# Another recorded order of the same items in a fused attention and two-layer kernel, and the warm-up matmuls in another PSUM bank

## The chip, the cores and the metric

The kernel runs on one core of a Trainium2 chip, as one program. The metric is the device time of one execution in microseconds (us); lower is better. PE is the matrix engine (TensorE), PEld its weight loads, DVE the vector engine, ACT the scalar engine, POOL is GpSimd, and SP is the engine that issues the DMAs.

## What is computed

Two steps follow each other. First attention with a hash mask, for 2 batches of 8 heads, 768 positions, 64 values a head:

```python
q_bits = (einsum('bhsd,dk->bhsk', q, proj) > 0)      # 6 bits a row, k_bits likewise
mask = q_bucket[:, :, :, None] == k_bucket[:, :, None, :]
scores = where(mask, matmul(q, k.T) / 8, -1e9)
attn = exp(scores - max(scores)); attn = attn / (sum(attn) + 1e-9)
x = matmul(attn, v)                                  # as 1536 rows of 512
```

Then two dense layers, each with weights of 512x2048 and 2048x512: `h = x @ w_in`, a pointwise `g(h)` (a clipped square in the first, `h - tanh(h)` in the second) and `x = g @ w_out`. The weights are wide (64 bits a value) in device memory and are made narrow in the kernel.

## The kernel before, in words

The 768 positions stand in two halves of 384 columns (SH). A query tile is 128 rows, so a group (one head, one half) has three tiles, and there are 96 tiles t, 48 for each batch. For one tile PE makes the scores with four matmuls of 384 columns (emit_s, lines 506 and 510), DVE takes their minimum (L524; the sign of the scores is turned) and makes bias and scale (L525), ACT makes the exponential and its sum (L526). Then the result is split into a high and a low fp16 part (L531 on ACT or DVE, L532 on POOL or L533 on DVE), a DMA transposes both (L537), and PE multiplies with V (pv, L631). For 18 of the 96 tiles PE itself transposes (turn, L593, evicted by L601) and multiplies in fp32 (L621). Each head's keys and queries are scaled and split before (L297 to L307), and their hash bits come from small matmuls into the bank PB, compared by DVE (first_k: L381, L382, L385; later heads L398, L399, L402; queries L412, L413, L416).

Every fp32 product is made of three matmuls with rounded operands: high by high, high by low, low by high. So each dense operand is split too: the high part by a copy on ACT or DVE (L300, L797, L815), the low part by a subtraction on POOL or DVE (L306 or L307, L798 or L799, L816 or L817). Raw weights are made narrow by L786 to L789. The dense products are L866 (bank pair MM); for batch 1 a Strassen-like form makes some from seven smaller products (products, L897, with sums on DVE L902 and weight sums on POOL or DVE, L811 or L810).

Nothing is issued while the program is being described. Every operation is put into a list (Plan.op) with the engines that may do it, and a recorded table, SCHEDULE, holds for each of the 3,456 items its place in the order and its engine. Plan.unpack reads the table, checks that no item stands before one that it depends on, and Plan.emit then issues the items in that order:

```python
for lo, hi in zip(code[:n], code[n:2 * n]):
    i = left.pop(lo + 256 * hi)
return out, [c[x][0] for x, (c, _) in zip(code[2 * n:], self.ops)]
```

Each engine works through its own items in that order and waits by semaphores for the others. Among the items are 64 that compute nothing (spin, L1127, here called spin items): four matmuls each of a constant tile `warm` into the unused last 128 columns of a PSUM bank, `WT` (L198). They keep PE busy where the order expects it to wait. The plan itself knows no dependency for them, but the framework puts a wait before a spin when another engine still works on the bank that it writes.

Of the kernel before, what the change touches and what calls it, by code (L numbers as in the profile page):

```python
# [20 lines left out]

SPINS = 64
SCHEDULE = (
    "c-rk)YjB*^d4At>Ki~bb`|Yk)yV_l8S6baAOO`Cz@)cw3*aXWsHsBbjiNO%sLP89QjlmcaJ7q!x851X5len&dB$Hd)q?sX^PEvO|40O_z>2xOf(LW_^r_-5E"
    "JMAz%qOL7lEA6@^{ZpUS=-WMe&Ux?8`<%UQ$H#CpZd<bxZr^wiuj98u2KVos`3JF?dYqyyNqQ5aW_grYwFp6{+p**|HPFCC&dvznUJPa0UIJ3EAnQsEX`8@A"
    "IgZ|)gfRJ!M2$hphpc$F9h^4)TdArM@opD{fDyK1C+@2_0<v9iJA3%!-M}D*H~A;aM2*>sWE>zVOqi0eC8Ds22ns7#G8<Q%rQ<K*@-wh{{KYftXHcve9mW;g"
    "c=EebQv^N$Y3DlFF!scHo7AcV)GccIk#*(D3X~v<Fgyuz2)dRnqlH|(t9>xrk)7%7g-ot{_np~bB$Gg8WFQ$TLuyaI*B{6A#EZJ)THG~+^_5--y+P5hwpF_P"
    "vgi999(Rpp%m#2#VLp^P&csQZ-WsJOrX3jw>V@2eh=qTc5{^&7w;TeN!u0RURPOZITq>X#dTHV#rP}`zc<}5=AG~M&w9OM)Ip^aPs6UQ=V2u9(p-}`5k=ASS"
    "ZqLIzU1cJ3M%%V{S0Q;(I{$Qs1Dx;H{G`Giw*>)v2Dxi<YFQ5fJxGZF6p>(TrI?<EbyIu|pZw7z`KbKia(U|tL_P{*y8_&~lLCS5+u4TzEHb;buSS4BCq7pZ"
    "9Pq@66R?h)1GXL?d-BQ0)_wNq41MIpr}5b1_(Jln%wx<!`jBN=IF1KL)EV{i5JmFN^Zod=Jb>bhpA!Igd=}{OrzrnR`XrM-|JgA{Pw+?I0Cw~U*+mZh<okzz"  # L30
    "N?vDx`0w9^2g#fN0-yLM0=)K*uWh}Ly~F<gSAWC&*WmPNAP)H@y!7%fQNv%W7vMSgDSV0ZXMfD`b)-74>7StfBP8;BKa_~y#x^E|2@#N2XrjJOT}jDV{#BVG"
    "v3!X|<X1HKazM$RFNWU9;OCCZeR%8bw>)s)c*D|fdiGzq=kmXB?YI8y+=N3X>_7jBH3lTDQiLogg!td*^t<vq4za&S`FDu0m=^6^r&tc~v>^OzuYQeyI4!6R"
    "ER!KhQJ2CqC-Lus;3XgQKf6Fq5YSxVqYl&7!=Mgv`>zg5{<a47Np7;3;Qa#bi}}3|5O|&5b@yFJ9AK_Ax%UZEkSN)!;`e}}5O4skXRl`(_9?m<$TpA?opxbU"
    "i$n4uBBf2mqvFUDhX{wQ?BLDAyJ6xtsUD!}qi{F>V0{|4_Uv={+B%GnGgv;=X{u#8fx*(qNP9;g(wUKd93s7wNJw?xShY$fMmhn<%h*pk0AOGYYJGXw(pBs3"
    "ht7eS^&2~BXAsPkC%d3D?iQD=BCb<d=1e&GVHn5`^!7o$AA0lwtv;Z;G#jf-!UU`xQCt?~aIvpX7WjZr*)3f5?Bv}-q(nztju|PIN+Agf(2@0%cAkb5bC~fv"
    "a})!2z@#ALqgkB`mBl>(d6o*M*uQ1lH%r>)Zn!4r3Y`eh@$_}_Z<QO9Uqs{MButNnbPJ~>u==F8o+@3l>5EiMtI0_qp_oAJjld`y8FEaK^lfnyLc*QonrM~~"
    "?}KaIb8Pi$V%s!toSo(Okh|Bg^!Wa9a>ulU(b3U2#mLY0JUl1_#Xso1@gRF}N1Z*e{p0Kgs9pc8I9a_%$fuu1!S`PaNWZoB3%4Kt#y5`B+g{bLyz&`+X73YJ"
    "8Mhqq-;w-~DfEZV@(0go=IYbVQ_MDLtY6rukB3B2$;9v2?5q5U>vH`mW5ub@Xm(Thg;S@#dF*EKd3J<z{v<oZ7^tskc;H2gJg?;=>eMOqFbKhs$%70jdmhP`"
    "#qlRzApDq_Gc$OYBO*CY4O*Re+(i4+cprA*(U*_u8;*j4=Z-)I;8QHMZ5!JP=`HueJ-6IT4wz!@3SeLRBm3ZX=zxO<AJj4fABG>@&-0S+h7=EOylW&PMxQKf"
    "CL~R;L#7dWxts;Did;W+%f_3N6|l?X{7tqU1Be}KW>v1XVe_6<>SoAH*%Gwc&31+D>_%vtis*EHQ+7po4QvR=_$cu@NKAt2Y_(1x*Ipe#kjrHW+I#gnSX=L*"  # L40
    "P^(b_HJ5kcGD<UK2z~<x3WZ*5kIT2!?(3=XS`BL)DxE;fG}qx!VmYa9TFbKZ`lyl~U^68`ix2hm&=MIO8%r1a6^*k4lydG<B7JICpxohbLNq0-dUMk527yK1"
    "HR9v$e7P)wAWJw_>-DK>wmX*@&oEZ0*eG?cq&@P62~SGesVlbD9r37MTQHpfbCMzNz7q*lDw{QQaUsgtk`SwNg0Dpur7~El#2P!4GTk=s4i|tE+aU%36%bJ>"
    "Bd5Z3x4I9cMAb`7gNzN91>luDTNWf*)0P00a27!*=@f($qumfFpRu7sI7rz|gS&dD=`Khr1VtzIr4VSkP^If=re}2zlrue1S5k~pseALiP-u&fLR(kVxnV=5"
    "vJTdF!$c|AIUej7D{kLW8ihj955w@|klhO|)ZiZIhJT%??LPodDeGg)0Dl__L-!69B&^T(5zc4&R`vBrIbECNhc}qd#<k~WT;Rh~4%y85`uk9i)-?`K4J$Q>"
    "<3eLy?Z=@_ID2?-BV9uW2JU1lKY}y#+9_J!OAbtQ6aJBLj$>?e#oo~oN{8s+ZFs9U?Cn`&s80`0+w~px<mg1T8^NhKlfzDFMDJQQtVgWbVQY3^I}FtO1_A1u"
    "px1P{YSFap4n|6)0wtu4lt*(pPBK9IFqfoo?p2R_qwW;eieXgg?2Iag7*(KX3Z&#Y09hN71Xh`<qQFfD6ls~3Aq44&`zosYA+NfcJKRE<S8YmZrBo`LS80@7"
    "q-n%y;4tc1j^i0R$F!D8qs&PZ8dBvn=Mc50ISW}pJ#YrV$TU1g)v1K`GReQ!Q_2YWG+;W;#c`CxkwMuuqZuVC3>8>5IF@6&kM@<9^%P4(-fp871Tpb#&nGSf"
    "j;~$Yu?<I2R)C4}QYd`@-{qkpE}q$oz0?4dFo|UPbdE5P#x*fPq)}TNgjs_!BISb1jft)?(sh-#yFisvN=J&ZwhljANTm`;On+k#QAFhi<-qMA9j;5-^Jw#|"
    "rI|@@#(~WQEP#~`owRKry%sZ&VhRsvi2)^y8uKVZWc(dEX!|Mi)DH6k+b}n`2v)n52Q<(wvPmY%WRiqt5?W&bot+p20YV}4JP)$5n;2q<9%^DE8s@>TH6}5F"
    "WF6v+39DgtuAwm0A|5gA$r?89HxvNO>2uNch-(&uVU<QVW+n_3jwxm!4$$yGQ;=xQt(L|t-X`YAtw}RlCJq+SNuya|1yK|*UouZvMPY-sG-Xm59t13*X$Hhl"  # L50
    "5#Nwa-}8Kp#<vxargumQl4lK20%SsPGa-SL?L}aPuH##C=LC-HxZuPZXg&zEZ@^rn(hj6zWU&Dp&lu%sXD;qe-X^&uYoP(7x%>mqP`gRPNCnknCbz2w)}WU`"
    "r)j4oA-u#4NeztAZs6uz&rL84(ILkF1``Zu87@>PF!SPhEV`7=C82SH38o|5lI;{7*F~Po=`1P(pQcqvCp66qCaD9$upe_Y<E%yu|1-Nu(fAl47eYQrXcDB9"
    "$xtsS#-0_n1)-7eDo~bD6y``gc$P~&i)t{jF_>ex6)<8>GHHtx&^0$08!VuP(51~58k*yc+U6gbi#QnIo%>|w%$314Sv~id`-8dn_}<*y<oR*&-Nh+){x_E_"
    "a4$ZcxrcM%8)x1sXW^O7lHWF3{$GFKII!5sO++?0)mc=jD>>%9f$(b`b_>Gs%2c!87h~-A%fbsXt^e%-^Cxhrx2=k^&abkXY<X{8YwGJoXZ4jV*DZTTUs$ah"
    "o~+^j(LlI5uDb5(xH_(mtK;gpI{vSlsA;2!O&V+SR!dsw*4XOWr4GQ$H6qxA9N;DQ5_~^MMe|kIx}5pf0Bn2^F1{UG(is;9{rpb+pV&DsXK=yA4;NU2i^pZr"
    "ELlu7T;N@7e9>wxScuJngN+nNSlq-$G8USRja0w}(Y;iSD~)zb&OltMTpMi1X7_z;APp~+FfQ1J3sba}pBJ!!1F@CR<K+&(#r%tlI0-M!)g{A^3lGJm0?;fe"
    "mq;#bHT@Ci#|ak~j;&`~gKTZhMGbs<Q4?%bhKnO&OYy(N{00)Sp;k+{23x7m#z^1tJ+`^+7bIYFzhk3t<HDkCgeI4#87>OXOBW=zn&#MAoUfp68rqAv1ovtE"
    "_XeB~cIP1vFEsK7c+fy8Yz@2dN=g(P5dp-7-4qd9X)_2*TXM0Qu;ET@X!ueNM{I#xK@&2CczMxcGlDRmg<%7df(sJma;}Q=LWNBuh6vcgs>a@JhO6gYfQ`}}"
    "F9|&^lAG8J=kUKpG@!EButPTIPuQ%-Hn8TrDwhKUVpE^~n#X?vH%h1Q"
)  # L60


# [65 lines left out]
def lsh_attention_moe_kernel(ctx: ExitStack, tc: tile.TileContext, qT, kT, vR, projR, eye, w1, w2, w3, w4, out, nbits):  # L128
    nc = tc.nc
    B, H, D, S = qT.shape  # L130
# [42 lines left out]
    P = [pall[:, i * S:(i + 1) * S] for i in range(3)]  # L173
# [17 lines left out]
    PV = bufs("pv", 1, [128, 512], F32, psum)  # L191
    PB = bufs("pb", 1, [128, 512], F32, psum)
# [11 lines left out]
    TF = [[krs.bitcast(F32)[:, i * SH:(i + 1) * SH] for i in range(4)],  # L204
          [vr[0].rearrange("p a b c -> p (a b c)")[:, i * SH:(i + 1) * SH] for i in range(2)] + [pt0[:, 2 * S + i * SH:2 * S + (i + 1) * SH] for i in range(2)]]
# [72 lines left out]
    NT = NG * TPH  # L278
# [440 lines left out]
    for k, (b, hs, l, qs) in enumerate(phases):  # L719
        n = 3 - len(hs)  # L720
# [17 lines left out]
    for w in range(NW):  # L738
        n = w % 3 if w < first_b1 else (w - first_b1 + first_b1 % 3) % 4
# [365 lines left out]
    t = HEAD  # L1105
# [71 lines left out]
```

## Time and profile before

| | |
|---|---|
| Median of 3 runs | 732.21 us (731.86 to 733.55) |
| Span of the profiled execution | 731.3 us (the page gives no other time of its own) |
| PE, PEld busy | 716.0 us (98%), 666.8 us (91%) |
| DVE, ACT, POOL busy | 629.3 us (86%), 480.6 us (66%), 343.9 us (47%) |
| DMA | 124.91 MB, mean 171 GB/s |
| Share of the chain that ended last | PE 86%, DVE 5%, DMA 4%, ACT 3% |

Read it by stages: PE is the busiest engine, but in the first quarter its busy time holds the spin items. Matmuls are pipelined, so a busy PE is not one at its peak: the distance from one start to the next is what a matmul costs, and a duration (some 335 ns for 384 columns) is longer than that.

### The profile page before, as it was taken

What the parts mean: (1) busy time and instruction counts of PE and PEld (TensorE: products, weight loads), DVE (VectorE), ACT (ScalarE), POOL (GpSimd) and SP (SyncE); (2) the same over time, 40 slices, a digit from 0 to 9 for tenths busy, and PEclk for the clock granted to TensorE, in tenths of its full rate; (3) what the DMA queues carried; (4) which work ended last, traced back from release to release, by engine and by line L of the source; (5) the groups of instructions that cost most, each with busy time, mean ns of one, the idle gap of its engine ahead of it and who ended that gap; (6) DMA issues with size and microseconds to landing.
All of it is one profiled execution on the core that took longest, in us unless ns stands there. A gap on an engine that the chain in (4) does not pass through costs nothing.

```text
span 731.3 us, 12554 instructions
## 1 busy us (share of the span) xinstructions
PE 716.0 (98%) x4512; PEld 666.8 (91%) x4512; DVE 629.3 (86%) x1063; ACT 480.6 (66%) x759; POOL 343.9 (47%) x244
## 2 busy tenths in 40 slices
PE   7899999999999999999999999999999999999998
PEld 6577789777999999999999999999999999999997
DVE  7998998988888999999788887988887898988774
ACT  7998898977978778778776777346544535524311
POOL 5874445565545536453445358541324415253430
PEclk9999999999999999999999999999999999999999
DMA  6997988999999798998888967632211311312112
GB/s 192 233 226 274 246 249 274 210 191 229 261 237 266 185 263 219 227 244 231 223 213 233 246 154 161 169 100 90 72 43 60 100 44 57 88 58 73 44 58 87
DMA packets 165102, 124.91 MB, mean 171 GB/s; under 512 B 127232, under 2 KB 135088, under 8 KB 165040
## 3 DMA queue, kind: packets, MB, share of 16 engines
q1 hardware_dynamic: 165040, 124.12, 65.1%
q8 instruction: 35, 0.57, 0.3%
q14 instruction: 27, 0.22, 0.1%
HBM read 73.47 MB, written 19.95 MB: 128 GB/s over the span
## 4 chain that ended last, share of the span: by engine, by line
PE 86%; DVE 5%; DMA 4%; ACT 3%; issue 1%; POOL 1%; SPq 0%; ACTq 0%; DVEq 0%; POOLq 0%
PE mm L866 52%; PE sbk L897 9%; PE pv L897 5%; PE pv L631 4%; PE ss L506 3%; PE ss L510 3%; PE pb L897 2%; DMA pt<-phl 2%; DVE sm L524 2%; PE pb L1127 1%; PE pv L621 1%; PE mm L593 1%; DMA vr<-in_v 1%; DMA pt<-tmp 1%; ACT p L526 1%
## 5 line engine op out<-in xcount | busy, mean ns | idle before, releaser
L798 POOL TENSOR_TENSOR wl<-wr,wh 128x512 fp32r<-128x512 f32 x69 | 96.0, 1398 | 124.8 <-ACT wh L797 62.2
L866 PE MATMUL mm<-gh,wh 128*128 128x384 f32 x396 | 107.2, 338 | 0.0
L866 PE MATMUL mm<-gh,wl 128*128 128x384 f32 x396 | 105.9, 335 | 0.0
L866 PE MATMUL mm<-gl,wh 128*128 128x384 f32 x396 | 105.8, 335 | 0.0
L526 ACT ACTIVATE p<-ss,sm 128x768 f32<-128x768 f32 x78 | 77.2, 989 | 39.9 <-DVE sm L525 38.4
L532 POOL TENSOR_TENSOR phl<-p,phl 128x768 f16<-128x768 f32 x41 | 70.5, 1720 | 53.6 <-DVE phl L531 20.1
L524 DVE TENSOR_REDUCE sm<-ss 128x1 f32<-128x768 f32 x82 | 78.2, 954 | 14.3 <-PE ss L510 12.2
L797 ACT ACTIVATE wh<-wr 128x512 fp32r<-128x512 f32 x91 | 56.6, 625 | 42.7 <-PE mm L866 23.7
L866 PEld LDWEIGHTS mm<-gh,wh 128*128 128x128 f32 x396 | 71.7, 188 | 1.0 <-issue 0.5
L866 PEld LDWEIGHTS mm<-gl,wh 128*128 128x128 f32 x396 | 72.2, 188 | 0.0
L866 PE MATMUL mm<-xh,wh 128*128 128x384 f32 x256 | 72.0, 341 | 0.0
L866 PEld LDWEIGHTS mm<-gh,wl 128*128 128x128 f32 x396 | 72.0, 188 | 0.0
L866 PE MATMUL mm<-xl,wh 128*128 128x384 f32 x256 | 70.6, 335 | 0.0
L866 PE MATMUL mm<-xh,wl 128*128 128x384 f32 x256 | 70.4, 335 | 0.0
L985 DVE TENSOR_TENSOR accs<-mm,accs 128x768 f32<-128x768 f32 x45 | 42.7, 951 | 9.3 <-PE mm L866 9.0
L306 POOL TENSOR_TENSOR gl<-tmp,gh 128x768 fp32r<-128x768 f32 x20 | 38.8, 1938 | 22.9 <-ACT gh L300 18.7
L789 DVE SCALAR_TENSOR_TENSOR wr<-w,wr 128x512 int32<-128x512 int32 x64 | 44.9, 708 | 4.4 <-ACT wr L787 2.4
L866 PEld LDWEIGHTS mm<-xh,wh 128*128 128x128 f32 x256 | 46.2, 188 | 1.9 <-issue 1.1
L799 DVE TENSOR_TENSOR wl<-wr,wh 128x512 fp32r<-128x512 f32 x59 | 43.8, 744 | 4.4 <-ACT wh L797 4.0
L866 PEld LDWEIGHTS mm<-xl,wh 128*128 128x128 f32 x256 | 46.8, 188 | 0.3 <-DVE xl L307 0.3
L866 PEld LDWEIGHTS mm<-xh,wl 128*128 128x128 f32 x256 | 46.7, 188 | 0.0
L631 PE MATMUL pv<-pt,v 128*64 128x384 f16 x468 | 41.7, 328 | 0.7 <-DMA pt<-tmp 0.7
(340 smaller groups left out, 1844.3 us busy)
## 6 DMA issues: line engine op xcount, KB each, us to landing
w<-in_w SPq DMA_DIRECT2D x64, 512.0 KB, 5.1
qr<-in_qT SPq DMA_DIRECT2D x32, 192.0 KB, 3.2
wr<-scr0i SPq DMA_DIRECT2D x24, 256.0 KB, 2.6
wr<-scr0o SPq DMA_DIRECT2D x24, 256.0 KB, 2.6
krs<-in_kT SPq DMA_DIRECT2D x14, 384.0 KB, 4.2
vr<-in_v SPq DMA_DIRECT2D x12, 384.0 KB, 5.2
scr0i<-wr SPq DMA_DIRECT2D x16, 256.0 KB, 5.0
scr0o<-wr SPq DMA_DIRECT2D x16, 256.0 KB, 3.0
```

Of the source, the lines that this page charges most:

```text
L306: op([("G", cg, lambda: G.tensor_tensor(dst, src, hi.bitcast(F32), op=ALU.subtract)), ("V", cv, lambda: V.tensor_tensor(dst, src, hi.bitca ...
L524: one("V", 870.0, lambda: V.tensor_reduce(z[:, 0:1], s, axis=AX.XY, op=ALU.min), cell, [c])
L526: one("A", 970.0, lambda: A.activation(halves(p), s, AF.Exp, bias=z[:, 2:3], scale=z[:, 3:4], accum_out=LS[lm][:, lk:lk + 1]), cell + [c], ...
L532: lo = [("G", 1600.0, lambda: G.tensor_tensor(hl[:, S:2 * S], p, hl[:, 0:S], op=ALU.subtract)), ("V", 870.0, lambda: V.tensor_tensor(hl[:, ...
L631: T.matmul(ps[j * 64:j * 64 + 64], v[:, kc, a, j, :], PT[n[j]][:, c * KC + kc, :], start=(kc == 0 and i == 0), stop=(kc == KC - 1 and i == 2))
L789: one("V", 600.0, lambda: V.scalar_tensor_tensor(wi, yi, 3, wi, op0=ALU.logical_shift_left, op1=ALU.bitwise_or), [("w64", i, 0)], [("wr", ...
L797: op([("A", 520.0, lambda: A.activation(whl(n)[0], WR[r], AF.Copy)), ("V", 335.0, lambda: V.tensor_copy(whl(n)[0], WR[r]), 1)], [("wr", r) ...
L798: op([("G", 1225.0, lambda: G.tensor_tensor(whl(n)[1], WR[r], whl(n)[0].bitcast(F32), op=ALU.subtract)), ("V", 600.0, lambda: V.tensor_ten ...
L799: ("V", 600.0, lambda: V.tensor_tensor(whl(n)[1], WR[r], whl(n)[0].bitcast(F32), op=ALU.subtract), 1)], [("wr", r), ("wh", n)], [("wl", n)])
L866: T.matmul(ps[:, s + hf, 0:SH], m[:, kc * 128:(kc + 1) * 128], y[:, hf * SH:(hf + 1) * SH], start=(kc == 0 and i == 0), stop=(kc == 3 and ...
L897: T.matmul(sbk(n), m[:, sl], v, start=(j == 0 and i == 0), stop=(j == 1 and i == 2))
L985: one("V", 870.0, lambda: V.tensor_tensor(a, ps, a, op=ALU.add), [pc], c)
```

## The change

Two things are changed. The recorded table is another one: the same 3,456 items with the same dependencies and candidate engines, in another order, and with another engine for some of those that may run on two or three. And `WT` lies in the bank PV (weighted values, written by L621 and L631 and read by L638) where it lay in PB (hash bits, small transposes, normalisers). Line numbers behind the table are lower by one.

```diff
 SPINS = 64
 SCHEDULE = (
-    "c-rk)YjB*^d4At>Ki~bb`|Yk)yV_l8S6baAOO`Cz@)cw3*aXWsHsBbjiNO%sLP89QjlmcaJ7q!x851X5len&dB$Hd)q?sX^PEvO|40O_z>2xOf(LW_^r_-5E"
...
+    "c-rk)X^frcRX*q4-}l>>yWcx^?ksm^d}r~@_|9sNJ>xC)Qtxr?CQYfbRBqw`H8D=&G-*;n8iN9LoHR>S3&(B2HKxI(P^Usd>JLDrpp^2X6@TC#5=cl95=8Kh"
...
     rts = sb.tile([2 * TPH, 256], F32, name="rts")
-    WT = PB[0][:, 3 * 128:4 * 128]
+    WT = PV[0][:, 3 * 128:4 * 128]
```

Counted over all items, DVE has 994 of them where it had 1,036, ACT 652 where it had 661, POOL 289 where it had 238; PE and SP keep their 1,140 and 381.

First place: PE at the second pair of hash-bit matmuls of the keys (pb: bank PB; ak, bk: split keys; ab: split queries; pw: split projection), from the end of the spin items ahead of it (`warm`) on, before:

```order
L1127 LDWEIGHTS warm
L1127 MATMUL pb_146<-warm 128x128
L381 MATMUL pb_146<-ak_68,pw 128x384
L382 MATMUL pb_146<-bk_70,pw 128x384
L506 MATMUL mm_143<-ak_68,ab_72 128x384 x2
L412 MATMUL pb_146<-ab_72,pw 128x384
L413 MATMUL pb_146<-ab_72,pw 128x384
L506 MATMUL mm_144<-ak_68,ab_72 128x384 x2
L506 MATMUL ss_150<-ak_68,ab_72 128x384 x2
L510 MATMUL ss_150<-bk_70,ab_72 128x384 x2
```

and in the change:

```order
L1126 LDWEIGHTS warm
L1126 MATMUL pv_145<-warm 128x128
L380 MATMUL pb_146<-ak_68,pw 128x384
L381 MATMUL pb_146<-bk_70,pw 128x384
L505 MATMUL mm_143<-ak_68,ab_72 128x384 x2
L1126 LDWEIGHTS warm
L1126 MATMUL pv_145<-warm 128x128
```

The last two rows of the change begin another spin item, ahead of the hash bits of the queries, where none stood. Counted along PE's order, the first burst has 36 spin matmuls where it had 56, and between the first two pairs of hash-bit matmuls stand 16 where 4 stood. Over the whole order all 64 spin items now stand ahead of the first multiplication with V, where 36 of them stood ahead of it before; the other 28 stood among later work.

Second place: DVE's first items behind the constants (krs, qr: raw keys and queries; ak, bk, ab: their split forms; sm: minimum, bias and scale of a tile), before:

```order
L298 TENSOR_SCALAR ak_68<-krs,cb 128x384
L307 TENSOR_TENSOR bk_70<-krs,ak_68 64x384 x2
L385 TENSOR_SCALAR bk_70<-pb_146,cb 12x384
L307 TENSOR_TENSOR ab_72<-qr_76,ab_72 64x384
L385 TENSOR_SCALAR bk_70<-pb_146,cb 12x384
L307 TENSOR_TENSOR bk_71<-krs,ak_69 64x384
L416 TENSOR_SCALAR ab_72<-pb_146,cb 12x384
L426 TENSOR_REDUCE vsm_80<-vr_78 128x1
L524 TENSOR_REDUCE sm_88<-ss_150 128x1
L525 SCALAR_TENSOR_TENSOR sm_88<-ss_150,sm_88 128x2
```

and in the change:

```order
L306 TENSOR_TENSOR bk_70<-krs,ak_68 64x384 x2
L384 TENSOR_SCALAR bk_70<-pb_146,cb 12x384
L306 TENSOR_TENSOR ab_72<-qr_76,ab_72 64x384
L384 TENSOR_SCALAR bk_70<-pb_146,cb 12x384
L306 TENSOR_TENSOR bk_71<-krs,ak_69 64x384
L415 TENSOR_SCALAR ab_72<-pb_146,cb 12x384
L306 TENSOR_TENSOR ab_73<-qr_77,ab_73 64x384
L523 TENSOR_REDUCE sm_88<-ss_150 128x1
L524 SCALAR_TENSOR_TENSOR sm_88<-ss_150,sm_88 128x2
```

The high part of the second key half (L298) has gone to ACT, and the reduction over V (L426) stands behind the first minimum of scores, no longer ahead of it.

Third place: DVE around the 48th minimum of scores, the last tile of batch 0 (sm_88 is its tile; rb, xl: the finished weighted values and their low part; phl: fp16 parts), before:

```order
L432 TENSOR_SCALAR vsm_83<-vsm_83 128x1
L799 TENSOR_TENSOR wl_111<-wr_106,wh_108 128x512
L524 TENSOR_REDUCE sm_93<-ss_150 128x1
L531 CAST phl_98<-p 128x768
L525 SCALAR_TENSOR_TENSOR sm_93<-ss_150,sm_93 128x2
L985 TENSOR_TENSOR accs<-mm_144,accs 128x768
L402 TENSOR_SCALAR bk_70<-pb_146,cb 12x384
L554 RECIPROCAL ls_95<-ls_95 128x6
L531 CAST phl_99<-p 128x768
L524 TENSOR_REDUCE sm_88<-ss_150 128x1
```

and in the change:

```order
L431 TENSOR_SCALAR vsm_83<-vsm_83 128x1
L637 TENSOR_TENSOR rb_96<-pv_145,rb_96 128x384
L523 TENSOR_REDUCE sm_93<-ss_150 128x1
L524 SCALAR_TENSOR_TENSOR sm_93<-ss_150,sm_93 128x2
L306 TENSOR_TENSOR xl_136<-rb_96,xh_128 128x384
L401 TENSOR_SCALAR bk_70<-pb_146,cb 12x384
L984 TENSOR_TENSOR accs<-mm_144,accs 128x768
L553 RECIPROCAL ls_95<-ls_95 128x6
L523 TENSOR_REDUCE sm_88<-ss_150 128x1
L524 SCALAR_TENSOR_TENSOR sm_88<-ss_150,sm_88 128x2
```

The two casts of fp16 parts (L531) and a low part of a weight (L799) have left this piece; the low part of finished values (L306 in the change) stands in it.

## Rows read from the trace of the kernel before

**Rows 1.** The page's part 1: busy us (share) x instructions of each engine.
```profile
PE 716.0 (98%) x4512; PEld 666.8 (91%) x4512; DVE 629.3 (86%) x1063; ACT 480.6 (66%) x759; POOL 343.9 (47%) x244
```

**Rows 2.** Busy time by stretch: stretch, length, PE, PEld, DVE, ACT, POOL, clock, DMA, GB/s.
```profile
0.00:42.00 42.00, 34.49 (x265) 26.47 (x267) 36.29 (x90) 36.84 (x57) 31.58 (x28) 1.00 0.86 218
42.00:100.00 58.00, 57.08 (x407) 44.91 (x404) 53.25 (x101) 50.95 (x84) 28.68 (x21) 1.00 0.94 248
100.00:183.00 83.00, 80.66 (x584) 66.07 (x583) 73.60 (x131) 69.76 (x119) 47.15 (x31) 1.00 0.92 229
```

**Rows 3.** The spin items' tile alone, by stretch: PE first, with its count.
```profile
0.00:42.00 42.00, 13.50 (x144) 10.86 (x144) 0.17 (x1) 2.62 (x4) 1.00 0.86 218
...
100.00:183.00 83.00, 7.68 (x88) 5.04 (x88) 0.00 (x0) 0.00 (x0) 1.00 0.92 229
```

**Rows 4.** Waits, 0 to 183 us: who waited for whom, us, times, longest.
```profile
DVE sm L524 <- PE ss L510: 5.0, 12, 1.0
...
ACT p L526 <- DVE sm L525: 9.3, 14, 1.6
```

**Rows 5.** Waits of PE, 200 us to the end; the only row.
```profile
PE mm L866 <- DVE accs L985: 1.1, 1, 1.1
```

**Rows 6.** Timeline of DVE, first items: start us, us, instruction, idle before.
```profile
4.64 1.01 DVE L307 TENSOR_TENSOR bk<-krs,ak 64x384 fp32r<-64x384 f32 x2
7.36 0.61 DVE L385 TENSOR_SCALAR bk<-pb,cb 12x384 fp32r<-12x384 f32 x1 [1.71 <-PE pb L382]
...
11.81 0.96 DVE L524 TENSOR_REDUCE sm<-ss 128x1 f32<-128x768 f32 x1
```

**Rows 7.** Timeline of PE: first burst of spins, first hash bits, a warm burst.
```profile
1.06 5.85 PE L1127 MATMUL pb<-warm 128*128 128x128 f16 x56 [1.06 <-DVE cb L254]
6.72 0.42 PE L381 MATMUL pb<-ak,pw 128*128 128x384 f32 x1
...
18.29 0.84 PE L1127 MATMUL pb<-warm 128*128 128x128 f16 x12
```

**Rows 8.** Timeline of DVE: the 48th minimum, and the eighth finished pair of heads.
```profile
162.44 0.96 DVE L524 TENSOR_REDUCE sm<-ss 128x1 f32<-128x768 f32 x1 [0.17 <-PE ss L510]
...
177.27 0.55 DVE L638 TENSOR_TENSOR rb<-pv,rb 128x384 f32<-128x384 f32 x1
```

**Rows 9.** Durations by line: xcount, min/median/max ns, first and last start.
```profile
L531 DVE CAST phl<-p x20: 550/557/847, 75.3 to 420.1; 128x768 f16<-128x768 f32 x20
...
L532 POOL TENSOR_TENSOR phl<-p,phl x41: 1643/1657/2104, 22.5 to 443.9; 128x768 f16<-128x768 f32 x41
...
L533 DVE TENSOR_TENSOR phl<-p,phl x28: 946/955/1770, 17.2 to 460.5; 128x768 f16<-128x768 f32 x28
...
L788 DVE TENSOR_SCALAR wr<-w x27: 411/420/607, 42.7 to 431.4; 128x512 int32<-128x512 int32 x27
...
L797 DVE CAST wh<-wr x37: 410/419/1396, 56.5 to 709.8; 128x512 fp32r<-128x512 f32 x37
...
L1127 PE MATMUL pb<-warm x256: 216/219/314, 1.1 to 182.4; 128*128 128x128 f16 x128
```

**Rows 10.** A group of DVE by shape: xcount | busy us, mean ns.
```profile
L799 DVE TENSOR_TENSOR wl<-wr,wh 128x512 fp32r<-128x512 f32 x59 | 43.8, 744 | 4.4 <-ACT wh L797 4.0
```

**Rows 11.** The chain that ended last, 128 to 183 us: start us, us, what.
```profile
141.71 6.33 DMA pt<-phl
...
160.83 5.11 DMA pt<-phl
```

**Rows 12.** The tail: PE's, DVE's and ACT's last splits; the same split on POOL elsewhere.
```profile
716.20 0.52 PE L866 MATMUL mm<-gh,wh 128*128 128x384 f32 x2
...
715.15 1.83 DVE L307 TENSOR_TENSOR gl<-tmp,gh 128x768 fp32r<-128x768 f32 x2
...
714.27 1.72 ACT L300 ACTIVATE gh<-tmp 128x768 fp32r<-128x768 f32 x2 [0.29 <-DVE tmp L940]
...
L306 POOL TENSOR_TENSOR gl<-tmp,gh 128x768 fp32r<-128x768 f32 x20 | 38.8, 1938 | 22.9 <-ACT gh L300 18.7 <-ACT p L526 2.3 <-DVE gh L300 1.8
```

More of the change, by code (lines that the diff above doesn't have):

````diff
@@ L28 @@
[L28 to L51, printed above, removed]
@@ new lines @@
+    "8#nf>*C3!EKhn&6-`wwg&wI{!&N<I_5hS46L0NztMsI)+bTuEazzV9c7is7t>FDs#m6cE#ET94wba5WeqcdOi$^ZeC*8v)H&c=)b@q6#RSNOO0fs=VXg73cj"
+    "F8Zt>DixrR(Qx8XsQ>+S5D|(s#OFVjJ`wpMY5xHy`eWG+hQXiDgT_L`;}r5`uSAP(;o5cV$WW~rCJ5ia?F=^HdeC6t;>C+NCYp#iGB>nNOdgoQ2~OiR+nE``"
+    "b(`syxw_giyBTC>cV=q(qt0yaBoTmJ)h?u!=0v4EtrkaFacC`~)4=TdLT(Cr(rl(PCADPjnq)BFJCq;v8adKOGWDTMV=xmYA?+)5_keE$QtJr8OFb{~Xy~>F"
+    "Sy?Hi?Rlq=n4Doc7bjXrk&gAOOx?r{0bFr43_WIuF*&9(#i+n!_*;=LgY-h``LV}dd7U|JEGQdt)^ol`b2OV8l4#%}NJI?aJn@XyPXwO|z)&h4F!BOAXz*Xe"
@@ new lines @@
+    "1^R|`T~~tm=kO&s%wG;eDXHhdZcdpbHeZCXU)jhxmhcfixn+(6K1iF*=Cs&JN8f&Xbo?Pca`fm?%7ETY2VjspdtLYN!LJcGw~OjM2rtUN!foOVC-`U2p94lp"
+    "ze(X)#HkEEH9?;I7MYwlHSwjVH9n=3Km3cAAES7JkmFxuh?Z#VSp7x)$yfCK=gu(pdHjv%fB2*41>=-I$3FVKd)Q}%c$%@No}tLTb&9c5<gK@^U6YT!N049U"
+    "_)nMqk>R8NaOL<{?N(odEq`rYo}{48|E&_Q$sfKBUwjq53+&}TF@Iss!dVBdU9;@`Lq*Pz<U3b20r`9ED*i72CTOB4{rbNP5~p7!N%H3TgfaF;_<H!``0rx!"
+    "3UQ<82S0*$-gzesne+V+g75!j@Inw!>J(K@=InaH2nj>;$A1ufhidYt-~J}^{VQ*WP5^kxBbNz<-*M5QKz`fj=jnMN4BC*siY_F{7tWr8@FfF*51yxfH3IOS"
@@ new lines @@
+    "^*r%(FDMS~XM{9TzsXO)Nn<|!2Bq^w%L!2L5ey#S;QgFo4&JBkr3xkRBQM}b?vv6Mt2lOSuOkG4VYo*r<=QKY?0R$5n1sTIm4Yc49oa6%$yz>SMv|F5s$Xk8"
+    "GpYR^xTiTa*PN7hk9Bu95!48bZyv_A^bqG8HVp7-w0&WGx_5ed{n(m<n5d7`kBCkoCWdpn_GO!*+NT>0=-u8on-UN5V!8(1L3_{)YJsVajg(4*Bhg-NxgYlR"
+    "hS1wTQ`f%env_u|gnqj(%20xSRv0zo{T0*GXL5~7NoIMjDj=()G}TN6YT}6rRZ{I<rI0Dj#NhyqqH(94rFlQ+$AvIThK92AsCH@D?d_%eLoZK6hv(_AprWlC"
+    "B4x~knBi47H{oW-$FoJ@<Ylrp+@{hkx&a^^*evG?1#gnLLEx^NNQ8H2_#h!eXZDq}!*^$P^+Wnu6!k<X<hx0`f716}{iTg+CMf;<dNn=$@bsr<ioZ6_y?>S9"
@@ new lines @@
+    "DyR8e^FGQ4M{EjD`%i*!5AHuHzN}(JJ6?P3weS8yw+dcXjt9rKZT+_UNA9oVIiZR=dnL@#ud7Ss%mL|o7e6Dfir}rQ!uO3Q=;fX9iJi`eXy(y3nbuwuF)z3r"
+    "s7s7}?h__?MqIdHvXOXOA9?%@5evD-4X(=H_pkWQ6?y6G?k~uP^@}DsCG-wKw2y+kDvrPMu#sQU7x^@o51i*T{L<$?@nt^vXuuwMRx-NlC1=a&)7-p3_46-K"
+    "5eN(C8Am+pAb;}ioKjDy{e0iaeR81iX=;mt94DmPdF~P2sqZht(+CfoKJ7l4gL|_d2fhOs6(S?xll<U=!KsHl{@4kCjIArBzQQS;<M<#8$V1r&GkfoU4n0Mp"
+    "on*)y6UcFk*f)q6Z2VY*`OuNz){|RZa^L{&&(y?mU1c#JnB<`E2PPTO8G6s4;zzc9#7;9!?)Enwv{S?FkbCXW(YtnyAvPMlo7Rl4DfP+T-E~HJGq-)yXb6PR"
@@ new lines @@
+    "T7`-<6qA!sA6JJVIE0k!WraO8wVUkRiL(mIP{=dk&=N&1cVVeAHzq)B*@jzLw&F5KyVUv*TONif+?6>j_|_`lyg#n+T(HZK^(057Qz7NKbar+&2{u+^Q}RQq"
+    "X?D}L?b|)~F-7L;TRUS@EY|wg)#CA~DIMxyYesi9+8rXCYM)cmekmFp7!jJRson)%V|`|g$F)-z3{+d3j3?QqH{5V+4`Kr($hQS`mvnWBROcQ2%WYZHW%^uG"
+    "vjd^c_%iENq$-shs8sIFU^qLw9^6B|p2#{bOEUe#2D&^QHKa0?L*u?_+O{<zYoZ5*XmnNj@>nakH+4ztE<MyNbqelg!nT2)HqLTUHYrx^fXkPrM_GJ0Je0TH"
+    "tJEkJq2OkduurEwX<Q9lr&;#fOT&)```c0H-9`?I1F~mpp<b}A<)`*c$xLlB{hRz|wN7oSNT>|Uq|{#=OURg*i$+F!dtt~-xy}&lZ}xvfAK%ez?mjZQU5^;z"
@@ new lines @@
+    "(bHvj<F<kR4ep2B*;%zoPW4V0ItF9uUAy^#;^=*&qsjK9ec#aGE#l*MZH{pVXH!AY8}&@~u#Mr&B<JfmQc9~ZOEyV4aG=yT!25;n>BruB1G+O3wm~~#R=>1S"
+    ">@Jo`$2cj{>hKUMQf_1kDGeeN26AbbZP<NiHxQ3tTbs$0%g|PWq|mE0=_E4s0li9@IOQ_;$S|r5O=UruD2ZYSMG#b_5N*WqJ%=cvQc;veH(y{8%kVVt;xyLT"
+    "m`9--Im}@$GsZJcw<)QdF7RBAL>ZdN#Wb)QFksSSt|wffYph6nsGTN+l=Fme`wJ41#(@`wN#rTa`hK4bf}Xk;qT7M0Ti2?NXB7t)Bw?tzGBm^}?1}}|q6)?V"
+    "?NDV@R-?=S0vQXm9c6?#h6OJ6c?be!op+;+t5qY+K2pg+wi1>ReDEWyLH&FLzCS-CyX&Fj@($DPChexe%Zj&^l|RHG?`D7|G-WD`LI!~m0*D=Hn4)zqn-XdV"
@@ new lines @@
+    "vKPQwbPaMxE8akjf@2>81~uNvfur@dV!IIfxe~?+Ko+7X>FtVK2x=Yeo~}Zr>b14evMLT5(0N6&z!E3zh|?OxP=Tlv1p)D;XU9G`)=g>~5m?QO^P<OWBnUI1"
+    "3}C|dW8lCH!XQW&g)zcTaf~Uqg3U&U5oNdFyg=;2tj7{Ub0mqZHM<1~gk}T;0miL5OBA(|juNQmJ#Zm*fU)^tMLu_ZcRsI<@QuT@?#L#ZLslj!#3?}PGW2{e"
+    "A^^&0s0w8WCrOQ$Ad3Kg#*!$`1yPLPg;C)8LG0R4Ko{8l(yk(74XIo{$FpFpFim=mC0*+2n&q^luHzI6zGIVbMV2CtRlDF5N4i!tL657ML|J33!}=pS2o#bw"
+    "s1$OXLYl`S#sSQq-FHK)#ZBGs_9LMMm~uG;Stv3PjAmFdNo|^95@LH4GvSxYp75>Qau5>0F{_WqjU|ywZ0>d6d=faX3lOFtZCV%uv@bB_T$)X@Q4~Og^S{eh"
@@ new lines @@
+    "5kt&#stDRoq$jP7j1-hgPcZ;3g{7)QLGxB|Q)!DhnkOwq%We(C77wN%No4=p%o79DYD~1c4d%rg+Q{At?*=}&{mI3Rdw?aEEZE?KPp#~q|GAD2{<9D_e?Fg^"
+    "g%@zk=S#1;`SE4U{44_hH!b4N;PL+FV)}p5w>!9lJGg^8xPv>mgFE<t0=%wA@fL0RQ-w-e*R15WlrOe;wk7WHwk_Yhf?x}R99Q)mms$3oQu(;lHMSHrY}pnr"
+    "=K$W!gO*;|@D~4Z(SwT*-1@s8w(`UZp~lv>xlJbGf-P~eftB|8$rm2D+ycZ_%k;nWE{V5Mc(~lTaKS+km#&4yyWN}?T#C5MhXGrq$I``(i`asQxR9Z^N=R`D"
+    "r?90w;8MxQh2^(msjgrHZ`m7hQTA{_!7kfev4y_4(g9cOVl9##7c>i85FuQh{J0GBR;#6jR&cfcxl9+r#hhEp?vmVJnNYY|Vs1Vfw%AzlmV+a<)FW`^jAN@6"
@@ L60 @@
+    "i!Cw>S11!)nN+yASue|9#FbBjt@Yn|lXw#i5P#ZmZuHMqV%$<Lu%#x5OO_wLf6|4`2^W=NE5ZX;Dkp>`>@E}D7QP;CdA={~{RlU^+fqL9MlP1%#Z5`Yg*CAB"
+    "{i->|TiQCVI`44x5<^@tCEoXFao%t1rJ;p!y@buhTv#NomaT@>>u#x5zu42&Thf2~m-PPuP%5^9"
 )
````

11 lines of the change are left out of this document (removed).

## Prediction

> **What bounds the kernel now.** I read the page first: PE is busy for 716.0 of 731.3 us [rows 1], and it has the same matmuls in both kernels. So nothing can be won but what PE spends waiting or on spin items. Where that lies is read from the busy time by stretch and from the same view for the spin items' tile alone. Up to the first multiplication with V, at 42 us, PE stands idle for 42.00 - 34.49 = 7.5 us, from 42 to 100 us for 0.9, and from 100 to 183 us for 2.3 [rows 2]; 144 of the 256 spin matmuls lie in the first of these stretches and 88 in the third [rows 3]. A warm one costs (0.84 - 0.22) / 11 = 56 ns, 0.22 us for an item of four: twelve of them take 0.84 us from the first start to the last end [rows 7]. The last starts at 182.4 us [rows 9], and from 200 us to the end PE waited once, for 1.1 us [rows 5]. The change can therefore win in the first quarter and hardly behind it.
>
> Who holds PE there? DVE and ACT are busy for 36.3 and 36.8 of 42 us, 53.3 and 51.0 of 58, 73.6 and 69.8 of 83, while POOL has half its time free behind 42 us [rows 2]. The waits decide between the two: ACT's largest is for DVE's bias and scale, 9.3 us; DVE's largest is 5.0 us, for scores [rows 4]. DVE is the nearer bound: a tile's minimum stands in its queue behind everything that was put ahead of it, ACT's exponential waits for that, and the transposition and PE wait for the exponential.
>
> **The change, part by part.** I take durations from the rows and counts from the two orders.
>
> *The queue of DVE up to the end of batch 0.* I count what stands in DVE's queue ahead of two landmarks: the 48th minimum of scores, which started at 162.44 us, and the product that finishes the eighth pair of heads, at 177.27 us [rows 8]. Setup left out, it is 262 items before and 255 now for the first, 283 and 274 for the second. For the second: gone are five splits L307 (three of half a tile at 0.5 and two of a whole at 0.92 [rows 6, 12], 3.4 us), three casts L531 (1.7) and two weight parts L799 (1.5) [rows 9, 10], four bit shifts L788 at 0.42 (1.7) [rows 9], and one each of L426, L466 and L976, which I take at the 0.95 of L533's whole tile (2.8); new are four evictions L601 (three whole tiles at 0.95, half a one at 0.55: 3.4), two L533 (1.9) [rows 9] and four small ones (1.5); L298 and L300 leave 0.5 less. That is 11.6 - 6.8 = 4.8 us less on DVE. The same count gives 3.7 us less for the 48th minimum. PE has one fewer dense item of 1.04 us (six matmuls) ahead of either landmark, which it must still do: so 4.8 - 1.0 = 3.8 and 3.7 - 1.0 = 2.7 us. I take the middle, **-3.2 us**. The ends are 0 (something else sets the pace, a rival below) and -5.7, if half of DVE's 5.0 us of waits for scores goes too. PE has room for it: 2.3 us idle and 88 x 0.056 = 4.9 us of spin items in that stretch.
>
> ACT's own queue ahead of its 48th exponential is 185 items for 187, 1.0 us less; behind it the three casts come back to it. Its 9.3 us of waits for DVE are its cover. If that cover were gone, ACT's relief of 1.0 us would set the term and PE's 1.04 us would cancel it, which is the zero end above.
>
> *POOL takes over.* Over the kernel DVE loses 42 items and ACT 9, and POOL gets 51. Ahead of the eighth pair POOL has 76 items for 70, some 7 us more, and 15 us idle in every 40 cover them [rows 2]. But the two engines are in each other's way: a cast L797 on DVE takes 0.42 us by its median and up to 1.40, a subtraction L533 0.96 and up to 1.77, and POOL's L532 1.66 and up to 2.10 [rows 9]. I charge one such collision of 0.3 to 0.8 us on the path: **+0.3 us**.
>
> The Trainium skill ("SBUF — State Buffer", Who interferes with whom) has DVE and GpSimd share one pair of ports under an exclusive lock, so that the loser waits for the whole instruction. The trace agrees in kind: the longest of those rows exceed their medians by 0.4 to 1.0 us, a good part of an instruction of the other engine. That speaks against moving work to POOL; rival 4 below prices it.
>
> *The head.* The first key matmul started at 6.72 us, behind 56 spin matmuls of 104 ns [rows 7], though DVE had made its operand by about 5.2 us [rows 6]. The first compare (L385) came at 7.36 us, after DVE had stood idle for 1.71 us [rows 6]. With 36 spins the burst ends at 1.06 + 36 x 0.104 = 4.8 us, and the data set the start. That frees some 1.5 us (6.72 - 5.2) at the first compare. The reduction over V (0.95 us) leaves the place ahead of the first minimum [rows 6], and another 0.54 us split comes in. Of this I count 1.3 us as lasting, since the shared chain of DVE goes on from there: **-1.3 us** (ends: 0 and -2).
>
> *The spin items and their bank.* All 64 now stand ahead of the first multiplication with V, 28 more than before: 28 x 0.22 = 6.3 us of PE time in a stretch where it idled for 7.5 us. I cost them at **0**, covered by that idle time; without the cover they cost up to 6.3 us, and that is the rival on the other side. In PB a spin could wait for DVE's reading of the hash bits and only then run, with the next matmul behind it; in PV, which nothing uses so early, it waits for no one. Before, twelve spins carried such a wait behind the first, so that is worth at most 12 x 0.22 = 2.6 us and is part of the cover, not counted twice.
>
> *Behind 183 us.* By the same count over the whole kernel DVE has some 26 us less and POOL some 60 more, so DVE has 21 us less behind 183; but PE hardly waited for it [rows 5], so **0** (ends: -1 and +2). The one wait of 1.1 us stands between the same two matmul items in both orders and stays. At the tail the second of the last two low parts goes from DVE to POOL, 1.94 us for 0.92 [rows 12]: its input is ready at 714.27 + 1.72 = 716.0, so it ends at 717.9. The new order puts twelve more matmuls of 0.174 ahead of its first use, which comes at about 716.20 + 14 x 0.174 = 718.6. Covered, by 0.7 us; without the cover it would cost 1 us.
>
> Sum: -3.2 + 0.3 - 1.3 = -4.2 us. From the span of 731.3 that is 727.1. The median of the runs lies 0.9 us above the span (732.21), so the time is **728.0 us**.
>
> **Rivals.** (1) *Transpositions set the pace, not DVE.* There are two buffers phl, and one comes free when its transposition has landed. Between 128 and 183 us the chain shows it: 6.33 and 5.11 us for one [rows 11]. With POOL's 1.66 us and the cast [rows 9] a buffer's cycle is 7.3 to 8.6 us, and nothing that DVE loses lies in it; three of the casts even go to the slower ACT. For it: these rows are on the chain. Against it: POOL's and DVE's waits make the rest of that stretch. Then DVE's relief and the head's are both waited away, and the time is about 731.5 us, no change. (2) *The spin items become the path.* Place: PE's queue up to about 18 us, where hash-bit and score matmuls stand behind bursts of up to 32 spin matmuls after the first. It decides if DVE has made its operand ahead of a burst's end. At the hash bits of the third group of queries PE has 36 cold and 116 warm spins and 14 pairs of matmuls behind it, so it gets there at 1.06 + 36 x 0.104 + 116 x 0.056 + 28 x 0.174 = 16.2 us at the earliest; DVE's 19 items ahead of it take 11.8 us from 4.5 us on, to 16.3 us. That is close, which is for this rival; against it, DVE will have waits on top of its 11.8. Price: the 6.3 us and the head's gain lost, 728.0 + 6.3 + 1.3 = 735.6 us, slower. (3) *PE's clock falls.* Between 100 and 183 us, 22 spin items lie in PE's waits; the change has none there. In the first burst the pace of 104 ns a matmul is that of 1.2 GHz, later 56 ns that of 2.4 GHz [rows 7], and the granted clock is 1.00 in the stretches of rows 2. The Trainium skill ("TensorE: Matmul & The Clock Gate", What's actually happening) says that the clock goes back to the lower level when the array has been idle; no stretch of this trace shows a fall. A stretch as long as the first burst loses 5.85 - 56 x 0.056 = 2.7 us, and two such would give 728.0 + 5.4 = 733.4 us. PE is 97% busy there [rows 2], spins included, so it is unlikely. (4) *Collisions of POOL and DVE.* If each of the six POOL items that are new ahead of the eighth pair held DVE up by 0.8 us, the longest L533 less the median [rows 9], the term would be 4.8 us in place of 0.3, and the time 732.5 us, no change. Against it: the medians lie within 20 ns of the minima, so most items meet none.
>
> **How the numbers follow.** Forecast 0.60; transpositions 0.14; spins on the path 0.17; clock 0.05; collisions 0.04. About 0.2% (1.5 us) is what a measurement of this kernel can tell from no change. So faster 0.60, the same 0.18 (rivals 1 and 4), slower 0.22 (2 and 3). The range goes from 723.5 (the far ends of the pace and the head and 1 us behind 183: 728.0 - 2.5 - 0.7 - 1 = 723.8) to 735.6 (rival 2); the forecast alone reaches from 723.5 to 730.7.
>
> **What would show it.** The 48th minimum of scores starting at 158 to 160 us where it was 162.44, and the eighth pair finished by about 173; the first compare L385 near 6 us; DVE's busy time some 25 us lower and POOL's 60 higher; PE idle below 6 us in the first 42 us; no spin behind the first multiplication with V. If the 48th minimum comes earlier but the eighth pair does not, rival 1 holds. If score matmuls start late with no wait shown and spins ahead of them, rival 2 does. More than 2 us of PE waits behind 200 us would make my zero there wrong.

## The result and the profile after

The changed kernel takes **739.85 us** (median of 4 runs, 739.09 to 740.22) against 732.77 us (731.86 to 733.55) for the kernel before on the same chip: a ratio of 1.0099, 95% interval 1.0085 to 1.0114. It is slower by 7.1 us (1.0%), where I forecast 728.0; my range ended at 735.6. The profiled execution took 739.09 us, with a span of 737.3.

The page's part 1 after, to be held against [rows 1] (line numbers are lower by one):

```profile
PE 716.7 (97%) x4512; PEld 667.8 (91%) x4512; DVE 628.5 (85%) x1021; ACT 476.7 (65%) x750; POOL 420.9 (57%) x295
```

PE does the same 4,512 matmuls in the same time and stands idle for 20.6 us where it was 15.3. **DVE has 42 instructions fewer and is busy for as long as before**, 628.5 against 629.3 us. POOL has 77.0 us more, not 60.

Busy time by stretch after (columns as in [rows 2]); then the last two stretches of the kernel before, which were not shown:

```profile
0.00:42.00 42.00, 39.13 (x382) 32.94 (x382) 34.67 (x83) 34.34 (x53) 28.96 (x27) 1.00 0.89 217
42.00:100.00 58.00, 54.03 (x370) 41.55 (x370) 53.14 (x103) 51.99 (x88) 38.77 (x27) 1.00 0.88 238
100.00:183.00 83.00, 76.39 (x494) 62.52 (x492) 72.74 (x124) 68.09 (x114) 47.55 (x32) 0.98 0.87 220
200.00:460.00 260.00, 258.61 (x1601) 245.84 (x1600) 235.21 (x355) 189.94 (x306) 147.59 (x97) 1.00 0.87 221
460.00:737.00 277.00, 271.67 (x1577) 268.50 (x1575) 216.92 (x334) 116.02 (x168) 146.96 (x106) 1.00 0.27 79
```

```profile
200.00:460.00 260.00, 259.98 (x1616) 248.37 (x1615) 228.52 (x363) 196.67 (x319) 130.84 (x90) 1.00 0.88 221
460.00:731.00 271.00, 266.79 (x1551) 263.96 (x1549) 223.37 (x359) 109.71 (x159) 96.06 (x71) 1.00 0.25 75
```

In the first 42 us PE's idle time falls from 7.5 us to 2.9, but spin items fill it. The spin items' tile alone after (columns as in [rows 3]):

```profile
0.00:42.00 42.00, 19.54 (x256) 16.70 (x256) 0.17 (x1) 1.04 (x2) 1.00 0.89 217
```

Of the 382 matmuls there 256 are spins, so 126 are the kernel's own, where it was 265 - 144 = 121 [rows 2, 3]. In every stretch behind PE loses: 4.0 us idle for 0.9, 6.6 for 2.3, and from 200 to 460 us 1.4 for none, with 15 matmuls fewer done in it (2.6 us at 0.174). In that stretch DVE is busy for 6.7 us more with 8 instructions fewer. My landmarks, from the order of DVE after:

```profile
5.87 0.61 DVE L384 TENSOR_SCALAR bk<-pb,cb 12x384 fp32r<-12x384 f32 x1
...
165.20 0.95 DVE L523 TENSOR_REDUCE sm<-ss 128x1 f32<-128x768 f32 x1
...
179.16 0.56 DVE L637 TENSOR_TENSOR rb<-pv,rb 128x384 f32<-128x384 f32 x1
```

The first compare came early, as forecast. The 48th minimum came at 165.20 us and the eighth pair at 179.16, where I had forecast 158 to 160 and 173; before they stood at 162.44 and 177.27 [rows 8]. Where did DVE's relief go? The groups by shape of DVE, first before, then after (count | busy us, mean ns | idle ahead):

```profile
L524 DVE TENSOR_REDUCE sm<-ss 128x1 f32<-128x768 f32 x82 | 78.2, 954 | 14.3 <-PE ss L510 12.2 <-ACT w L786 0.9 <-ACT xh L300 0.2
L789 DVE SCALAR_TENSOR_TENSOR wr<-w,wr 128x512 int32<-128x512 int32 x64 | 44.9, 708 | 4.4 <-ACT wr L787 2.4 <-ACT w L786 1.2
L788 DVE TENSOR_SCALAR wr<-w 128x512 int32<-128x512 int32 x27 | 11.5, 427 | 0.4 <-POOL wl L798 0.2
```

```profile
L523 DVE TENSOR_REDUCE sm<-ss 128x1 f32<-128x768 f32 x82 | 78.3, 954 | 20.6 <-PE ss L509 19.0 <-ACT v L467 0.4 <-ACT wh L796 0.3
L788 DVE SCALAR_TENSOR_TENSOR wr<-w,wr 128x512 int32<-128x512 int32 x64 | 56.7, 891 | 2.3 <-ACT wr L786 1.5 <-ACT w L785 0.4
L787 DVE TENSOR_SCALAR wr<-w 128x512 int32<-128x512 int32 x24 | 14.6, 609 | 0.3 <-DMA w<-in_w 0.2
```

The minima take 954 ns in both kernels. The same 64 bit operations on weights take 11.8 us more, and 24 shifts take more than 27 did. Eight microseconds of the timeline after, DVE first and then POOL, show how:

```profile
386.89 1.50 DVE L787 TENSOR_SCALAR wr<-w 128x512 int32<-128x512 int32 x1
388.49 1.97 DVE L788 SCALAR_TENSOR_TENSOR wr<-w,wr 128x512 int32<-128x512 int32 x1
...
391.99 1.44 DVE L788 SCALAR_TENSOR_TENSOR wr<-w,wr 128x512 int32<-128x512 int32 x1
393.44 0.96 DVE L523 TENSOR_REDUCE sm<-ss 128x1 f32<-128x768 f32 x1
```

```profile
386.82 1.28 POOL L797 TENSOR_TENSOR wl<-wr,wh 128x512 fp32r<-128x512 f32 x1 [5.58 <-ACT wh L796]
388.06 1.85 POOL L531 TENSOR_TENSOR phl<-p,phl 128x768 f16<-128x768 f32 x1
391.23 1.65 POOL L531 TENSOR_TENSOR phl<-p,phl 128x768 f16<-128x768 f32 x1 [1.32 <-ACT phl L530]
```

Each of the two operations of L788 starts while POOL works and ends 0.55 us after POOL does (390.46 against 389.91, and 393.43 against 392.88); the tile's minimum waits behind the second. Summed over DVE, the time above the median of the same operation and shape (where it is over 0.1 us) is 24.4 us in 50 instructions before, and 52.4 us in 82 after; every one of these instructions, in both traces, overlaps an instruction of POOL. I had counted some 26 us of relief at medians; these 28.0 us take it back.

How such a delay reaches PE, five rows of four engines after:

```profile
455.43 1.31 POOL L797 TENSOR_TENSOR wl<-wr,wh 128x512 fp32r<-128x512 f32 x1 [0.25 <-POOL gl L305]
455.52 1.77 DVE L788 SCALAR_TENSOR_TENSOR wr<-w,wr 128x512 int32<-128x512 int32 x1
457.22 0.94 DVE L523 TENSOR_REDUCE sm<-ss 128x1 f32<-128x768 f32 x1
458.45 0.99 ACT L525 ACTIVATE p<-ss,sm 128x768 f32<-128x768 f32 x1 [1.36 <-DVE sm L524]
459.59 0.62 PE L505 MATMUL ss<-ak,ab 128*128 128x384 f32 x2 [0.36 <-ACT p L525]
```

DVE's operation takes 1.77 us where its median is 0.69, and again ends 0.55 us after POOL's. The minimum stands behind it in DVE's queue, the exponential waits for the minimum, and PE's next scores wait for the exponential, which frees their bank. Nobody in this chain reads what POOL made.

### The profile page after: what moved, and what is told of

Same layout as the page of the kernel before. It is cut to its first block, busy times and chain, and to the rows that moved or that the text cites. A ratio compares the mean times of both kernels' runs of the same rounds, so it can differ in the third digit from the quotient of the medians.

```text
span 737.3 us, 12567 instructions
## 1 busy us (share of the span) xinstructions
PE 716.7 (97%) x4512; PEld 667.8 (91%) x4512; DVE 628.5 (85%) x1021; ACT 476.7 (65%) x750; POOL 420.9 (57%) x295
## 5 line engine op out<-in xcount | busy, mean ns | idle before, releaser
L797 POOL TENSOR_TENSOR wl<-wr,wh 128x512 fp32r<-128x512 f32 x86 | 121.1, 1413 | 102.9 <-ACT wh L796 48.1
L531 POOL TENSOR_TENSOR phl<-p,phl 128x768 f16<-128x768 f32 x44 | 76.3, 1735 | 60.2 <-ACT phl L530 41.7
L523 DVE TENSOR_REDUCE sm<-ss 128x1 f32<-128x768 f32 x82 | 78.3, 954 | 20.6 <-PE ss L509 19.0
L796 ACT ACTIVATE wh<-wr 128x512 fp32r<-128x512 f32 x83 | 51.3, 624 | 46.1 <-PE mm L865 16.0
L305 POOL TENSOR_TENSOR gl<-tmp,gh 128x768 fp32r<-128x768 f32 x25 | 49.0, 1963 | 27.7 <-ACT gh L299 25.7
L788 DVE SCALAR_TENSOR_TENSOR wr<-w,wr 128x512 int32<-128x512 int32 x64 | 56.7, 891 | 2.3 <-ACT wr L786 1.5
L530 ACT ACTIVATE phl<-p 128x768 f16<-128x768 f32 x54 | 45.0, 834 | 3.6 <-DMA pt<-phl 3.3
L785 ACT ACTIVATE w<-w 128x512 f32<-128x512 f32 x64 | 42.0, 666 | 3.9 <-DVE vr L658 2.6
```

Of the source, the lines that this page charges most:

```text
L305: op([("G", cg, lambda: G.tensor_tensor(dst, src, hi.bitcast(F32), op=ALU.subtract)), ("V", cv, lambda: V.tensor_tensor(dst, src, hi.bitca ...
L523: one("V", 870.0, lambda: V.tensor_reduce(z[:, 0:1], s, axis=AX.XY, op=ALU.min), cell, [c])
L530: hi = [("A", 730.0, lambda: A.activation(hl[:, 0:S], p, AF.Copy)), ("V", 470.0, lambda: V.tensor_copy(hl[:, 0:S], p), 1)]
L531: lo = [("G", 1600.0, lambda: G.tensor_tensor(hl[:, S:2 * S], p, hl[:, 0:S], op=ALU.subtract)), ("V", 870.0, lambda: V.tensor_tensor(hl[:, ...
L785: one("A", 560.0, lambda: A.activation(y, y, AF.Prelu, scale=2.0**-112, alpha=-(2.0**32)), [], [("w64", i, 0)])
L788: one("V", 600.0, lambda: V.scalar_tensor_tensor(wi, yi, 3, wi, op0=ALU.logical_shift_left, op1=ALU.bitwise_or), [("w64", i, 0)], [("wr", ...
```

## The experiments

Theory A: POOL, given more work, holds DVE up, mainly behind 183 us. Theory B: the early spin items and the clock. Tables of order were written anew as each expectation says, and line numbers shift by a few. All ratios are to the kernel before on the same chip.

**Halves of the change.** Spin items at their old places, in PB (the diff is against the change):

```diff
 SCHEDULE = (
...
 )
-    WT = PV[0][:, 3 * 128:4 * 128]
+    WT = PB[0][:, 3 * 128:4 * 128]
```

> The changed order and engine choices, but the 64 spin items stand behind the same PE items as before, and their bank is PB again. Theory A (POOL and DVE hold each other up behind 183 us, where the changed engine choices give POOL more): the loss stays, 737.5 us or more, with the four PE waits at about 320, 400, 458 and 476 us. Theory B (the early spin items, and PE's falling clock where they are missing at 140 us): about 732 us or less, and the granted clock is 1.00 from 140 to 150 us.

Measured: **756.68 us**, 1.0327 (1.0310 to 1.0345), far above A's bound of 737.5 us and B's 732. PE in the first 42 us and two of its waits there:

```profile
0.00:42.00 42.00, 30.14 (x198) 22.34 (x198) 29.59 (x74) 29.27 (x44) 23.43 (x23) 0.83 0.76 186
```

```profile
PE pb L412 <- DVE bk L385: 2.4, 2, 2.1
...
PE pb L1127 <- DVE cb L254: 1.1, 1, 1.1
```

Most of this loss is in the head: PE waits more there, the granted clock was 0.83, and the spins stand behind matmuls of another order. The last row is no cost of this order: it is the first burst's wait for the constants, which the kernel before has too [rows 7]. Behind 200 us three of the change's waits of PE stayed (1.3 us), and the fourth was 0.4 us for 1.0.

Old order with the new engines, and the reverse (the table's last third exchanged, nothing else):

> The order and spin places of before with the engine choices of the change. Theory A: 4 us slower than before, about 737 us, with 40 us or more of DVE time above the medians (24 before, 52 in the change). Theory B: no difference from before, 732 to 733 us. Theory C (the order alone is worse, whatever the engines): also no difference.

> The changed order, spins and bank with the engine choices of before. Theory A: the 4.5 us behind 183 us come back and the 1.5 us ahead of it stay, about 735 us. Theory B or C: as slow as the change, about 740 us.

Measured: **808.72** (1.1009 to 1.1057) and **844.66 us** (1.1501 to 1.1534). Every expected time missed by tens of microseconds. A's other sign, 40 us or more of DVE time above the medians, came in the first (101.7 us), but in a kernel too disturbed for it to count. An order is a plan for particular engines. That with others each queue meets its operands at the wrong time is my reading; the traces show PE's waits, with 18.4 and 14.8 us for the exponentials alone. These two say nothing about A's share of the 7.1 us; cutting by time does.

The change's table up to the PE item of 190 us, then the rest as before; and before up to 190 us, then the rest as the change has it:

> Order and engines of the change up to the PE item that started at 190 us in it, and behind that the rest in the order and with the engines of before. Theory A (4 us or more of the loss arise behind 183 us, from what the change gives POOL there): 734 to 735 us. If the loss came from the head alone: 739 us.

> The reverse: before up to 190 us, then the rest as the change has it. Theory A: 736.5 to 738 us, with waits of PE near 320, 400, 458 and 476 us. If the loss came from the head alone: 733 us.

Measured: 742.32 us (1.0109 to 1.0139) and **736.94 us**, 1.0057 (1.0045 to 1.0069). The second is what A gave: 4.3 us of the 7.1 arise behind 190 us, in a kernel whose head is the old one. The first lost 5 us right behind its seam, by PE's position in its own work, missed both expectations, and tells nothing of either half.

**The spin items and the bank.** Only the spins moved early, in the old kernel:

```diff
-    WT = PB[0][:, 3 * 128:4 * 128]
+    WT = PV[0][:, 3 * 128:4 * 128]
```

> The order and engines of before; only the 64 spin items stand where the change puts them, all ahead of the first multiplication with V, in bank PV. Theory A: within 2 us of before (731 to 735 us). Theory B: the whole loss, 736 us or more, with the granted clock below 1.00 in the waits of 140 to 183 us, where before had spin items. If the head gains as I forecast and nothing is lost, 731.5 us.

Measured: 733.35 us, 1.0007 (0.9998 to 1.0016), no change. PE by stretch:

```profile
0.00:42.00 42.00, 36.60 (x356) 31.52 (x357) 35.37 (x82) 34.32 (x53) 29.75 (x26) 0.98 0.84 209
42.00:100.00 58.00, 56.65 (x390) 42.48 (x389) 53.65 (x103) 51.32 (x85) 30.28 (x23) 0.99 0.91 243
100.00:183.00 83.00, 77.94 (x508) 64.16 (x506) 75.33 (x136) 72.17 (x122) 47.89 (x32) 1.00 0.94 234
```

Theory B falls: what the spins no longer fill behind 100 us becomes idle time (5.1 us for 2.3 [rows 2]), and the first compare, at 5.99 us for 7.36, gains nothing in the end. The change with only its bank undone (the diff of e1, with the table kept):

> The change with one thing undone: the spin items write bank PB again. If the bank does nothing: 739.8 us. If a spin item in PB has to wait for DVE's reading of that bank, as one row of the first experiment shows (1.1 us), up to 20 us slower, with the granted clock low in the first 42 us.

Measured: **744.21 us**, 1.0174 (1.0145 to 1.0203): in this order PV is worth 4.4 us by the medians and 5.5 by the ratios. The spins in PB wait for DVE's reading:

```profile
PE pb L1126 <- DVE bk L384: 2.4, 4, 0.8
PE pb L1126 <- DVE xl L401: 2.1, 2, 1.1
PE pb L1126 <- DVE ab L415: 2.0, 3, 1.3
```

The 1.1 us that the expectation took from e1 was not such a wait but the one for the constants; the rows here are. Order, engines and bank are those of e1, whose spins stand at their old places: against its 756.68 us the early places are worth 12 us.

Fewer of them (45 and 14 in the kernel before, 36 in the change):

```diff
-SPINS = 64
+SPINS = 45
```

> The kernel before without the 19 of its 64 spin items that stand behind the first 100 us of PE's own work (136 us and later). Theory E (PE executes the spin items where it would else wait, and what they fill is set by the chain through DVE, ACT and the transposing DMAs): 4.2 us of spin time go, and waits of 3 us or more come in their place, 730.5 to 733 us. Theory F (the spins are simply PE's path there): 728.5 us. If the clock falls without them: 733 us or more, granted below 0.997 in the mean.

> The change with 36 spin items in place of 64: every second one behind the first nine is gone. If the 28 extra ones stood on the path in the head: 6 us less, 734 us. If idle time covered them, as I forecast: 739 to 740 us. If PE's clock falls in the head without them (as in the first experiment, where it was 0.83): slower than the change.

> The kernel before with its first burst of 14 spin items and none behind. Theory E: 730 to 733 us, the spins' time turned into waits. Theory F: 722 us (50 items of 0.22 us less). If the clock falls: 736 us or more.

Measured: 734.27 us (1.0009 to 1.0031), 739.25 (1.0062 to 1.0093) and 732.68 (0.9991 to 1.0008). Taking 50 of 64 away changes nothing, so theory F falls. Taking 28 of the change's away gives 0.6 us by the medians and 1.5 by the ratios, whose intervals overlap. Taking 19 away cost 1.4 us: that fits only the third case by its time, and its sign, a mean clock below 0.997, came in 2 of the 10 runs; it stays unexplained. With 14 spins PE idles for 5.1 us in the stretch where it had 2.3 us of idle time and 4.9 us of spins:

```profile
100.00:183.00 83.00, 77.91 (x508) 64.73 (x507) 75.29 (x135) 72.25 (x122) 47.66 (x31) 1.00 0.94 234
```

**The clock.** Ten spins of the change moved into PE's wait of 2.5 us:

```diff
-    def spin():
+    def spin(bank):
...
-            T.matmul(WT, warm, warm, start=True, stop=True)
+            T.matmul(bank[0][:, 3 * 128:4 * 128], warm, warm, start=True, stop=True)
...
-        one("PE", 300.0, spin, [], [])
+        one("PE", 300.0, lambda bank=PV if n < SPINS - 10 else PB: spin(bank), [], [])
```

> The change, with ten of its spin items moved from the stretch ahead of the first multiplication with V into PE's wait of 2.5 us at 141 us (these ten write PB, the others PV). Theory: PE's clock falls behind that wait (granted 0.52 from 144 to 147 us in the change) and costs 1 to 2.5 us; with the wait filled, the granted clock is 1.00 there and in the mean, and the time is 737.5 to 739 us. Rival: the clock costs nothing, since PE is waited for by nobody there: 739.8 us.

Measured: 739.16 us, 1.0087 (1.0072 to 1.0102), which the interval can't tell from the change. The stretches around the wait, in the change and then here:

```profile
140.00:147.00 7.00, 4.35 (x17) 3.81 (x16) 5.83 (x11) 5.26 (x9) 6.54 (x5) 0.76 0.94 181
147.00:183.00 36.00, 32.42 (x222) 25.69 (x220) 30.44 (x52) 29.16 (x49) 20.86 (x15) 1.00 0.89 192
```

```profile
140.00:147.00 7.00, 6.49 (x64) 5.83 (x62) 6.22 (x13) 5.78 (x8) 6.07 (x5) 1.00 1.03 223
147.00:183.00 36.00, 32.51 (x213) 25.83 (x213) 31.82 (x50) 28.33 (x49) 20.67 (x15) 0.95 0.85 182
```

The filled wait kept the clock up, and it fell at a later one instead.

**Does DVE's queue set the pace up to 183 us?** From here on instructions named in a set work on a part of their columns (the diff is that of the second run below; the first cuts the exponentials to one half):

```diff
         for i in out:
+            Short.on = i in SMALL
...
+    def cut(self, *aps):
+        return [a[:, 0:32] for a in aps] if Short.on and len(aps[0].shape) < 4 else aps
```

> The kernel before, with the exponentials of the 25th to 48th tile of scores over one half of their columns (384 of 768); the other half of p stays stale. Theory C (from the 25th tile on there is one buffer for scores, so scores, minimum, exponential and the next scores follow one another, some 3.5 us a tile, and neither DVE's nor ACT's queue sets the pace): 0.3 to 0.4 us less a tile, the 48th minimum 7 to 9 us earlier, and 726 to 729 us in all. Theory D (my forecast: DVE's queue sets the pace): ACT is not what is waited for, 731.5 us or more.

> The kernel before, with 32 instructions of DVE on the weights between 73 and 178 us (bit shifts, casts, low halves; 20.1 us) cut to 32 columns, the rest of the weights stays stale: some 16 us less in DVE's queue, none of it in the loop of scores, minimum and exponential. Theory D: the 48th minimum comes 5 us or more earlier, 726 to 729 us. Theory C: only what stood right ahead of a minimum counts, at most 2 us: 730.5 to 732.5 us.

Measured: 731.77 us (0.9983 to 1.0001) and 731.88 us (0.9981 to 0.9998). The first refutes C, since the 48th minimum came at 163.66 us and not 7 to 9 us earlier; the second refutes D, since the time fits C's side. So neither theory is left. The 48th minimum in the second, where DVE was busy for 12 us less (617.4 us in all; I had expected 16):

```profile
161.15 0.96 DVE L561 TENSOR_REDUCE sm<-ss 128x1 f32<-128x768 f32 x1 [0.67 <-PE ss L547]
```

1.3 us earlier than before, and waiting for PE. Most of that is within what two executions of one head differ by: e6, with the head of before, has it at 161.34 us. PE's own items fill that stretch to 94% even without spins (77.91 of 83 us above), so no single queue has more than the rest to give.

**POOL's added work behind 183 us.** 42 instructions that the change moved from DVE to POOL, and the control in the kernel before:

> The change, with 42 instructions that it moved from DVE to POOL between 183 and 466 us (65.9 us of POOL's time) cut to 32 columns; what they leave out of the low halves stays stale. Theory A (DVE is held while POOL works, so its minima come late): DVE's busy time between 200 and 460 us falls from 235 by 6 us or more, PE's waits at 320, 400 and 458 us go, and the time is 735.5 to 737 us. Rival (the order of the queues is at fault, not POOL's time): 739 us or more.

> The control for the short POOL instructions: the kernel before, with 42 of POOL's instructions between 183 and 466 us (59.5 us) cut to 32 columns. If what the same cut won in the change was the loss that the change had brought there, nothing is to be won here: 732 to 733 us. If the cut wins by itself (less traffic, fewer waits everywhere), 729 us or less.

Measured: **735.61 us**, 1.0040 (1.0025 to 1.0055), and 733.10 us, 1.0007 (0.9998 to 1.0016). The cut wins 4.2 us in the change and nothing before: most of the loss behind 183 us is POOL's added work. (Two of e8's six runs had a mean granted clock of 1.000 and none of the change's; at 0.998 the spans are 733.8 and 733.9 us for 737.3, so 3.4 us.) Which part of it? The twelve that lie in a tile's own chain, and the other thirty:

> The change, with only the 12 subtractions of the probabilities (phl) that it moved to POOL between 183 and 466 us cut to 32 columns (20.4 of the 65.9 us); the low halves stay stale. Theory A (DVE is held while POOL works): these stand beside some 3.3 of about 10 us by which DVE's instructions are held there by the 42, so a third of the 4.2 us comes back: 738 to 739 us. Rival G (the tile's own chain is longer through POOL): nearly all of it, 736 us.

> The change, with only the other 30 of the 42 instructions (low halves of weights and operands, two additions; 45.5 us) cut to 32 columns. Theory A: two thirds come back, 736.5 to 737.5 us, and DVE's busy time between 200 and 460 us falls by 4 us or more from 235.2. Rival G: 739 us or more.

Measured: 738.11 us (1.0051 to 1.0088) and 738.28 (1.0049 to 1.0108); by time they can't be told apart: the first lies where theory A had it, the second above A's 737.5, and the runs of e17 alone lie between 735.23 and 742.53. The stretch from 200 to 460 us tells them apart, in the order e8, e16, e17, e12:

```profile
200.00:460.00 260.00, 259.95 (x1614) 248.14 (x1614) 226.76 (x359) 191.01 (x309) 103.79 (x99) 1.00 0.88 221
```

```profile
200.00:460.00 260.00, 259.00 (x1603) 246.21 (x1602) 232.30 (x356) 190.29 (x309) 132.54 (x97) 1.00 0.88 220
```

```profile
200.00:460.00 260.00, 259.85 (x1611) 247.48 (x1610) 228.97 (x360) 192.06 (x310) 116.89 (x98) 1.00 0.89 220
```

```profile
200.00:460.00 260.00, 259.98 (x1616) 248.38 (x1615) 224.79 (x365) 196.44 (x318) 88.88 (x90) 1.00 0.89 221
```

Of the 15 matmuls lost in that stretch the thirty give 10 back and the twelve in a tile's chain 2; DVE's busy time falls by 6.2 and 2.9 us. Of PE's 2.3 us of waits from 200 to 500 us in the change none is left in e17 and 1.7 us in e16, and no wait of PE in the change is put down to POOL. So rival G falls: instructions whose results PE is not seen to wait for cost the time, through DVE. These counts are of one execution each.

The same for POOL's 11 weight parts between 100 and 180 us:

> The change, with POOL's 11 subtractions of weights between 100 and 180 us (14.7 us) cut to 32 columns. If DVE being held beside them (some 3 of 4.5 us there) is the early part of the loss: the wait at 141 us gets shorter by 1 us or more, the 48th minimum comes at 163 us or before (165.2 in the change), and the time is 737.5 to 738.5 us. If not: 739 us or more, the 48th minimum at 164.5 us or later.

Measured: 737.82 us, 1.0068 (1.0051 to 1.0084). The time fits; the steps only in part. The wait at 141 us was 2.2 us in place of 2.5, and the 48th minimum came at 164.22:

```profile
PE pb L462 <- DVE vsm L461: 2.2, 1, 2.2
```

```profile
164.22 0.96 DVE L559 TENSOR_REDUCE sm<-ss 128x1 f32<-128x768 f32 x1
```

That is 1 us by the landmark, no more than two executions of one head differ by (162.44 us before, 161.34 in e6). Nor does the hold set the wait at 141 us: the two weight operations of DVE ahead of it took 0.77 and 0.69 us for 1.51 and 1.01, but then DVE waited 0.41 us for scores, and the reduction that PE waits for started 0.1 us earlier. The 2 to 3 us lost in the first 183 us have no cause that these runs show.

## Why the prediction was wrong, step by step

**The queue of DVE: -3.2 us, measured +1.9 to +2.8 at the two landmarks.** The step that failed is "that is 11.6 - 6.8 = 4.8 us less on DVE", priced at the medians of the kernel before and taken to be the pace. Neither held. Between 100 and 183 us DVE's instructions ran 4.4 us above their medians (1.4 before), and cutting 20.1 us of DVE's own work to 32 columns moved the 48th minimum by 1.3 us and the time by under 1 (e11). "DVE is the nearer bound", read from the sum of its waits, did not hold: eased alone, neither DVE's nor ACT's queue gave 1 us. PE had 2.3 us idle there, 5.1 with every later spin gone (e15). "PE has room for it" counted spin time as room, and it turned into waits (e4, e13).

**POOL takes over: +0.3 us.** Right in kind, wrong in size and place. I looked at the collisions ahead of the eighth pair and charged one. Rival 4 capped them at 4.8 us, "no change". They lie behind 183 us: 47.0 of the 52.4 us (22.7 of 24.4 before). The rule that I quoted from the Trainium skill ("SBUF — State Buffer", Who interferes with whom) says that the loser waits for the whole instruction; the rows at 388 and 392 us agree, with 0.55 us of work after POOL's end. Measured over the kernel and not for one item, it takes back the whole relief. Its size could hardly have been read from the trace before: 24.4 us beside 343.9 us of POOL, scaled to the 77.0 more, is 5.5 us (an estimate), and it was 28.0.

**Behind 183 us: 0 (ends -1 and +2), measured +4.3** (e6). This is the term that decided. "DVE has 21 us less behind 183" did not come: from 200 us to the end it is busy for 452.1 us where it was 451.9, with 33 instructions fewer, and from 200 to 460 us for 6.7 us more. With POOL cut short 4.2 us come back (e8). PE's waits, none from 200 to 500 us before, are now:

```profile
PE ss L505 <- ACT p L525: 1.3, 3, 0.5
PE pv L896 <- DVE rb L637: 1.0, 1, 1.0
```

That is 2.3 us, over the 2 that I had named as the sign; the rest of the 4.3 stands in no wait that the view shows.

**The head: -1.3 us, measured 0.** The first compare did come 1.5 us earlier, at 5.87 us. The gain did not last: in e4 it came at 5.99 us, with the order of before, and the time was 733.35 us.

**Spin items: 0, measured 0.** Taking 28 out of the change's head gave 0.6 us by the medians, with intervals that overlap (e14), so rival 2 with its 6.3 us does not hold. The bank was undervalued: I gave PV at most 2.6 us, and it is worth 4.4 in this order (e7), because in PB the spins wait for DVE's reading of the hash bits.

**Rival 3** happened in part, though I called it unlikely. Behind the wait at 141 us the granted clock is 0.76 over seven microseconds. (The trace before has such a stretch too, which I missed: 0.96 in its last 11 us.) In the six runs of e8 the spans are 732.7 and 732.8 us at a mean clock of 1.000, 733.8 and 733.9 at 0.998, 734.7 and 735.6 at 0.995: 1 to 3 us, against the 2.7 a fall that I had. In e14 they are 735.0 and 735.8 us at 1.000 and 737.2 to 738.8 below. All four runs of the change stood at 0.998 or 0.995, so a part of its early loss may be the clock's. What causes what is not shown: in e15, at 0.990 to 0.995, the time is that of before, and filling one wait (e9) moved the fall and left the time inside the interval. **Rival 1** was not tried by itself. That the head, the exponentials, the spins and DVE's queue can each be eased for under 1 us fits a chain that shares out its waits, of which the transpositions are a part; it stays open.

The wait of 1.1 us between the two matmul items stayed, as costed (the view puts it down to ACT now). Of the other signs, PE's idle time in the first 42 us (2.9, below 6) came as named; DVE's busy time (25 us lower) and POOL's (60 higher) did not, and they were the ones to trust. The low end of my range was 723.8 us by its own sum, not 723.5.

## What to carry to other kernels

Work moved to a second engine is not priced by its medians when the two hold each other up. Sum, over the whole kernel, how long instructions run above their median while the other engine works, and charge that to the engine that others wait for; here it cancelled all of the relief. The sum in the trace before is not the price: here it more than doubled. An order and its choice of engines are one plan: exchange them together or cut by time. And the room for a gain is the idle time of the engine that ends last, not the spin items that it executes.

## What was not expected of the hardware

Not every DVE instruction was held. The 82 minima over PSUM took 954 ns in both kernels, with POOL 10% of the span busier, and none took over 960; the bit operations in SBUF went from 708 to 891 ns. Spin items of 0.22 us each moved to the head for nothing in the old order (e4); in the new one they cost 4.4 us more in the bank PB (e7) and another 12 at their old places (e1). PE's clock fell behind waits of about 2 us in some executions and not in others (the change 0.76 from 140 to 147 us around a wait of 2.5 us, e8 1.00 around one of 2.2 us). The granted clock of the first 42 us reads 1.00 before and after, though the first burst ran at 104 ns a matmul and later ones at 56 [rows 7]: that column alone would not have shown the slow burst.
